# A new instruction order for the last three quarters of a fused attention and SwiGLU block

## The chip, the cores and the metric

The kernel runs on one core of a Trainium2 chip. The metric is the device time of one execution in microseconds (us). The kernel before was run three times: 239.23, 239.26 and 241.12 us, median 239.26.

A core has five engines that run their own instruction queues strictly in the order in which they were written and wait for each other through semaphores: TensorE (PE in the profile, with its weight loads as PEld), VectorE (DVE), ScalarE (ACT), GpSimd (POOL) and SyncE (SP), which here issues nearly all DMAs.

## The reference

2048 rows of 512 numbers pass an attention half and a feed-forward half, each with a layer norm that is scaled and shifted by a condition vector, and a gated residual:

```python
mod = (_silu(c) @ w_mod).reshape(c.shape[0], 6, 1, -1)
sa, ca, ga, sb, cb, gb = ...
h = _layernorm(x, axis=-1) * (1 + ca) + sa
x = x + ga * _A_ref(h, A_wqkv, A_wo)
h = _layernorm(x, axis=-1) * (1 + cb) + sb
x = x + gb * _B_ref(h, B_w1, B_w3, B_w2)
```

`_A_ref` is attention with 32 heads of 16, in which a row sees itself and seven earlier rows at a distance of 2, 4, ... 14. `_B_ref` is a SwiGLU: `(silu(h @ w1) * (h @ w3)) @ w2` with 1792 inner columns.

## The kernel before

The 2048 rows are 16 tiles of 128 (T = 0 to 15). The kernel is a list of 1118 operations, each with its engine, its instructions and what it reads and writes (`_build`, from line 273). Two lists at the end of the file say everything about their sequence. `ORDER` (line 980) has the operations' numbers in one global order; `Program.place` (line 143) deals them out to the five engines in that order, so it fixes each engine's queue. `SLOTS` (line 1027) has the buffer of each value that takes one from a pool: one of eight PSUM banks, or one of a few buffers for queries, normalized rows, shifted values, attention weights, FFN products and so on. From both, `Program.synchronize` (line 165) derives every semaphore wait: an operation waits for what it reads, and for the last users of the buffer that it takes over. A change of the two lists therefore moves operations within the queues and changes waits, and leaves each operation as it is.

The operations that the text names, by tile or row group:

- **lg T** (TensorE, line 752): 16 small matmuls that sum the products of query and shifted keys to logits, with the array split in four; VectorE makes the products before (**pq T**, line 742, 2.28 us).
- **at T** (TensorE, line 807): transposes of the softmaxed weights of tiles T and T+1; the softmax itself is some VectorE steps and an Exp on ScalarE.
- **value loads** (SP, line 124 in the profile, like every DMA): four DMAs of 256 KB for each tile bring the values, shifted by the eight distances, from a scratch in DRAM.
- **av T** (VectorE, line 827, 2.28 us): values times weights. **ac T** (TensorE, line 855): eight split matmuls that sum them; ScalarE copies the sum to SBUF (line 861), and a DMA, **ot T**, transposes it.
- **wo T** (TensorE, line 867): output projection, four matmuls; VectorE adds it to x (line 871).
- **second layer norm**: GpSimd and ScalarE (lines 586 to 601). For tiles 0 to 3 TensorE transposes the normalized rows (line 636). For the others a DMA transposes each tile (`sb_h<-sb_xn`) and four ScalarE instructions modulate a group (line 621).
- **F g.u** (TensorE, line 883): four matmuls with w1 (the gate) or with w3 (the other factor) for inner column block u (0 to 13) of row group g. Groups 0 and 1 are tiles 0-1 and 2-3, groups 2 and 3 tiles 4-7 and 8-11, groups 4 and 5 tiles 12-13 and 14-15; a matmul has 256 columns in groups 0, 1, 4, 5 and 512 in 2 and 3. ScalarE takes the SiLU (line 889), VectorE the product (line 892).
- **Z halves** (TensorE, line 921; line 909 for tiles 14 and 15): seven of the 14 matmuls with w2 of a tile; VectorE adds x (line 931) and SP stores the tile.

TensorE has enough independent work of the FFN to fill the time in which attention steps of other tiles wait for VectorE, ScalarE or a DMA. Which F or Z stands between which attention steps is written in `ORDER` and nowhere else.

Of the kernel before, what the change touches and what calls it, by code (L numbers as in the profile page):

```python
# [272 lines left out]
def _build(p, A_x, A_wqkv, A_wo, B_w1, B_w3, B_w2, c, w_mod, out):  # L273
# [720 lines left out]
    604, 311, 312, 269, 303, 317, 318, 386, 387, 309, 310, 388, 304, 401, 418, 605, 307, 308, 606, 389, 390, 607, 609, 608, 337,  # L994
    278, 315, 392, 313, 314, 322, 325, 445, 225, 338, 615, 610, 614, 616, 394, 611, 393, 613, 612, 305, 391, 328, 306, 329, 443,
    316, 444, 405, 406, 319, 617, 622, 626, 407, 446, 627, 395, 396, 397, 419, 420, 623, 477, 45, 634, 635, 447, 642, 618, 272, 320,
    46, 636, 637, 628, 629, 619, 620, 621, 52, 226, 326, 51, 630, 631, 408, 624, 625, 344, 638, 448, 421, 422, 50, 640, 639, 641,
    662, 670, 644, 643, 645, 449, 409, 646, 410, 450, 632, 647, 47, 633, 654, 398, 399, 451, 663, 666, 400, 671, 672, 452, 48, 343,
    650, 655, 668, 667, 669, 648, 649, 682, 683, 684, 453, 652, 651, 653, 435, 656, 657, 664, 433, 436, 685, 454, 665, 673, 658,
    678, 434, 437, 321, 426, 686, 687, 689, 695, 688, 694, 691, 660, 323, 659, 661, 423, 478, 475, 696, 424, 438, 425, 697, 690,  # L1000
    692, 674, 693, 742, 439, 730, 465, 731, 466, 468, 743, 427, 744, 745, 726, 706, 708, 707, 709, 476, 479, 467, 469, 428, 458,
    429, 710, 711, 456, 457, 712, 713, 722, 723, 724, 727, 728, 729, 455, 732, 733, 440, 725, 430, 746, 698, 699, 459, 53, 702, 703,
    480, 54, 470, 471, 472, 734, 735, 441, 442, 460, 461, 345, 346, 714, 431, 432, 738, 762, 462, 481, 497, 482, 473, 474, 483, 675,
    676, 747, 763, 463, 464, 704, 498, 484, 764, 765, 499, 715, 487, 716, 717, 700, 701, 718, 720, 509, 770, 771, 679, 705, 750,
    736, 737, 490, 748, 772, 485, 719, 500, 749, 488, 721, 739, 740, 752, 741, 507, 766, 767, 769, 489, 779, 768, 751, 754, 753,
    486, 501, 773, 774, 778, 775, 776, 780, 777, 781, 782, 491, 785, 758, 759, 760, 327, 783, 755, 529, 502, 510, 508, 492, 784,
    798, 818, 511, 512, 503, 531, 532, 680, 830, 493, 513, 330, 530, 831, 521, 539, 832, 514, 515, 820, 822, 814, 799, 815, 522,
    819, 504, 505, 516, 517, 541, 494, 324, 520, 495, 518, 506, 834, 806, 786, 807, 496, 761, 836, 794, 833, 823, 835, 677, 821,
    838, 858, 808, 859, 681, 533, 534, 559, 519, 523, 535, 809, 837, 540, 558, 542, 543, 524, 860, 525, 570, 790, 796, 795, 788,
    797, 545, 861, 791, 810, 787, 789, 802, 792, 793, 526, 544, 536, 547, 546, 549, 548, 862, 537, 569, 538, 550, 803, 527, 528,  # L1010
    839, 863, 864, 804, 805, 811, 551, 594, 812, 813, 866, 824, 825, 867, 800, 567, 593, 552, 553, 554, 874, 592, 868, 869, 826,
    557, 816, 560, 801, 840, 827, 870, 871, 555, 872, 568, 556, 817, 876, 841, 865, 854, 875, 561, 873, 846, 877, 828, 571, 842,
    595, 881, 562, 572, 829, 577, 563, 584, 855, 879, 578, 579, 564, 573, 850, 856, 580, 574, 878, 880, 906, 908, 581, 596, 565,
    566, 575, 576, 954, 857, 585, 907, 583, 909, 918, 919, 894, 582, 586, 843, 956, 955, 957, 886, 887, 958, 756, 898, 587, 588,
    895, 597, 890, 891, 589, 926, 847, 598, 599, 959, 960, 962, 899, 900, 901, 927, 961, 848, 590, 600, 591, 601, 1032, 910, 920,
    921, 963, 964, 965, 892, 893, 967, 966, 1034, 928, 1033, 1035, 1036, 1037, 851, 968, 852, 849, 972, 974, 976, 978, 973, 980,
    929, 911, 984, 986, 977, 979, 975, 844, 845, 985, 987, 853, 1039, 988, 990, 989, 1038, 930, 931, 932, 981, 982, 983, 933, 902,
    904, 991, 903, 905, 970, 934, 969, 1040, 896, 897, 971, 882, 1041, 888, 889, 884, 883, 922, 885, 923, 935, 936, 924, 946, 1043,
    1042, 942, 937, 938, 950, 1004, 1006, 1005, 1007, 1000, 1045, 1002, 1001, 925, 1008, 1012, 1009, 1013, 1016, 1017, 996, 998,
    997, 914, 999, 915, 1018, 992, 1003, 1044, 993, 994, 1014, 1015, 1019, 995, 916, 757, 912, 917, 1024, 913, 939, 1028, 940, 1070,  # L1020
    1090, 1071, 1086, 1072, 1073, 1091, 1010, 1087, 1074, 1011, 1082, 1075, 1088, 941, 1083, 1078, 1089, 1079, 1092, 1093, 1094,
    1084, 1096, 1095, 1097, 1080, 1081, 943, 951, 1085, 952, 944, 947, 948, 949, 1054, 1050, 1066, 1051, 1052, 1053, 953, 945, 1020,
    1062, 1064, 1076, 1077, 1063, 1046, 1067, 1068, 1069, 1047, 1055, 1056, 1057, 1021, 1022, 1023, 1058, 1060, 1059, 1061, 1029,
    1048, 1025, 1098, 1049, 1030, 1065, 1099, 1100, 1101, 1110, 1111, 1112, 1114, 1115, 1113, 1116, 1117, 1026, 1027, 1102, 1031,
    1103, 1104, 1105, 1106, 1107, 1108, 1109,
]
SLOTS = [
    7, 0, 1, 2, 3, 4, 5, 6, 0, 1, 2, 3, 4, 5, 6, 7, 0, 1, 2, 3, 4, 5, 6, 7, 0, 3, 4, 5, 6, 0, 1, 1, 0, 2, 3, 0, 4, 0, 7, 1, 0, 2, 1,
    2, 3, 6, 1, 5, 0, 7, 5, 7, 6, 2, 2, 1, 4, 0, 1, 3, 1, 2, 0, 4, 1, 4, 0, 7, 5, 1, 3, 6, 3, 0, 4, 2, 0, 1, 2, 1, 1, 0, 2, 4, 0, 1,
    2, 1, 4, 3, 6, 5, 1, 1, 0, 1, 3, 2, 3, 2, 4, 0, 0, 2, 3, 4, 1, 0, 3, 5, 6, 5, 1, 5, 3, 3, 2, 2, 0, 2, 6, 1, 2, 0, 3, 6, 7, 5, 3,  # L1030
    0, 1, 1, 0, 6, 0, 1, 1, 0, 0, 0, 0, 0, 1, 1, 5, 1, 6, 0, 1, 1, 1, 0, 5, 1, 0, 3, 1, 5, 0, 2, 3, 1, 4, 0, 2, 4, 2, 100, 5, 1, 2,
    5, 1, 1, 0, 1, 4, 0, 7, 1, 0, 4, 0, 1, 1, 1, 1, 5, 0, 7, 0, 0, 1, 1, 6, 0, 1, 1, 1, 0, 5, 1, 0, 0, 100, 7, 0, 2, 1, 1, 6, 0, 2,
    6, 2, 100, 5, 1, 1, 3, 1, 3, 0, 2, 5, 0, 4, 1, 0, 0, 1, 0, 1, 6, 0, 0, 6, 1, 0, 4, 1, 7, 0, 2, 6, 6, 1, 0, 0, 1, 1, 6, 100, 2,
    0, 0, 2, 1, 4, 7, 2, 1, 5, 103, 2, 102, 3, 101, 6, 103, 1, 100, 4, 101, 5, 104, 2, 106, 4, 102, 3, 100, 3, 105, 2, 104, 1, 102,
    4, 105, 1, 100, 3, 108, 5, 104, 2, 109, 4, 105, 7, 110, 5, 102, 7, 113, 5, 103, 6, 111, 2, 102, 6, 107, 6, 101, 1, 112, 0, 100,
    3, 102, 0, 3, 2, 0, 4, 4, 104, 0, 101, 1, 105, 1, 102, 1, 105, 7, 115, 1, 103, 4, 116, 7, 100, 2, 100, 5, 101, 7, 105, 7, 101,
    5, 119, 2, 102, 1, 117, 7, 100, 7, 118, 5, 103, 2, 103, 4, 100, 5, 106, 5, 104, 4, 114, 2, 102, 0, 104, 6, 104, 4, 107, 2, 101,
    0, 101, 2, 1, 4, 3, 1, 1, 105, 5, 113, 3, 100, 1, 100, 6, 101, 0, 112, 1, 103, 5, 115, 3, 101, 1, 101, 6, 100, 5, 110, 6, 100,
    7, 102, 0, 102, 1, 116, 4, 101, 5, 109, 3, 104, 6, 105, 3, 101, 5, 103, 0, 105, 7, 108, 4, 105, 0, 111, 7, 105, 7, 119, 1, 103,
    3, 100, 5, 102, 4, 103, 0, 1, 2, 4, 2, 3, 105, 5, 108, 6, 103, 7, 105, 6, 105, 4, 114, 4, 102, 1, 115, 7, 101, 4, 106, 7, 100,  # L1040
    4, 113, 7, 100, 0, 104, 7, 104, 1, 114, 1, 100, 4, 113, 7, 104, 0, 107, 6, 100, 1, 116, 0, 100, 3, 117, 0, 101, 3, 110, 2, 102,
    4, 109, 7, 100, 3, 102, 0, 101, 5, 103, 0, 3, 0, 6, 101, 0, 103, 2, 101, 0, 100, 4, 105, 5, 118, 2, 100, 1, 102, 3, 100, 7, 101,
    4, 105, 5, 112, 4, 103, 6, 108, 2, 100, 4, 119, 4, 103, 6, 104, 6, 101, 2, 111, 2, 105, 1, 100, 4, 102, 1, 105, 1, 101, 2, 106,
    3, 103, 0, 113, 2, 102, 6, 100, 1, 2, 1, 0, 102, 3, 116, 1, 103, 5, 118, 4, 104, 5, 110, 7, 100, 4, 114, 0, 101, 1, 117, 7, 105,
    7, 109, 4, 102, 4, 115, 7, 100, 5, 107, 7, 102, 1, 108, 4, 104, 7, 112, 7, 103, 1, 101, 1, 101, 4, 102, 1, 105, 4, 103, 5, 105,
    0, 100, 3, 101, 6, 103, 7, 101, 4, 103,
]


# [26 lines left out]
```

## Time and profile before

| | us |
|---|---|
| median of three runs | 239.26 |
| the profiled execution | 240.36 |
| its span | 238.6 |
| TensorE busy | 232.2 |
| VectorE busy | 179.4 |
| ScalarE busy | 138.3 |
| GpSimd busy | 28.8 |
| TensorE idle from 36 to 236 us | 2.05 |

The page divides the span into 40 slices of 6 us and gives the busy share of each in tenths. A timeline lists instructions of one engine in the order of time, like ones merged, with the engine's idle time before them in brackets and what ended it. Ends of matmuls are modelled, so a merged row's length runs a little past the start of the next one; distances are taken from start to start. For SP a row is the time of issuing; the landing comes later. Times in the text count from the start of the span.

### The profile page before, as it was taken

The numbers are of one execution on the slowest core, as the hardware profiler recorded it, in microseconds if no ns is written. First come the engines' busy times: TensorE is split into PE (matmuls) and PEld (weight loads), VectorE is DVE, ScalarE is ACT, GpSimd is POOL, SyncE is SP. The second block draws the span as 40 slices with busy tenths as digits, with TensorE's granted clock in tenths as the row PEclk, the third lists the DMA queues.
The fourth block names the chain that finished last, engine by engine and source line by source line (L and its number), as shares of the span: only waits on it lengthen the run. The fifth ranks groups of instructions, "written<-read, shape, count | busy, mean of one in ns | idle before, by whom it ended". The sixth has DMA issues, their size and how long they took to land.

```text
span 238.6 us, 4560 instructions
## 1 busy us (share of the span) xinstructions
PE 232.2 (97%) x1806; PEld 136.7 (57%) x1806; DVE 179.4 (75%) x279; ACT 138.3 (58%) x267; POOL 28.8 (12%) x66
## 2 busy tenths in 40 slices
PE   7999999999999998999999999999899999999995
PEld 4776554545688683664444444444375457485874
DVE  5699999999999999899999999690653403434433
ACT  2289587899978737776765594747553406040300
POOL 4434000013002000240003420020010000000000
PEclk9999999999999999999999999999999999999999
DMA  6999999999999996876972783634303000000202
GB/s 216 372 330 309 157 242 301 217 288 315 302 293 254 247 203 178 240 180 193 229 220 62 192 209 76 166 113 46 67 5 104 3 0 0 3 22 0 69 1 88
DMA packets 46317, 38.85 MB, mean 163 GB/s; under 512 B 21704, under 2 KB 37080, under 8 KB 46296
## 3 DMA queue, kind: packets, MB, share of 16 engines
q1 hardware_dynamic: 46288, 38.56, 65.1%
q8 instruction: 14, 0.23, 0.4%
q14 instruction: 7, 0.06, 0.1%
q10 hardware_dynamic: 8, 0.00, 0.0%
HBM read 29.62 MB, written 4.21 MB: 142 GB/s over the span
## 4 chain that ended last, share of the span: by engine, by line
PE 83%; DMA 8%; DVE 3%; SPq 3%; ACT 1%; issue 0%
PE pall L883 40%; PE pall L921 17%; PE pall L691 7%; PE pall L867 5%; DMA sb_x<-in_A_x_dram 5%; PE pall L711 4%; DMA sb_ot<-sb_ac 3%; PE pall L752 3%; SPq L124 3%; PE pall L855 3%; PE pall L909 3%; DVE sb_pq L742 2%; DVE sb_st L555 1%; PE pall L807 1%; DVE sb_xn L576 1%; ACT sb_ac L861 0%
## 5 line engine op out<-in xcount | busy, mean ns | idle before, releaser
L883 PE MATMUL pall<-sb_h,sb_w 128*128 128x256 bf16 (+1 forms) x672 | 102.6, 308 | 0.0
L883 PEld LDWEIGHTS pall<-sb_h,sb_w 128*128 128x128 bf16 x672 | 65.0, 98 | 35.7 <-issue 2.5
L889 ACT ACTIVATE sb_sg<-pall 128x256 bf16<-128x256 f32 (+1 forms) x84 | 35.6, 454 | 54.5 <-PE pall L883 53.4
L892 DVE TENSOR_TENSOR sb_hh<-sb_sg,pall 128x256 bf16<-128x256 bf16 (+1 forms) x84 | 40.0, 505 | 36.1 <-PE pall L883 34.0
L921 PE MATMUL pall<-sb_w,sb_hh 128*128 128x512 bf16 x196 | 44.9, 379 | 0.0
L742 DVE TENSOR_TENSOR sb_pq<-sb_q,sb_kT 128x4096 bf16<-128x4096 bf16 x16 | 36.3, 2282 | 0.0
L921 PEld LDWEIGHTS pall<-sb_w,sb_hh 128*128 128x128 bf16 x196 | 19.0, 98 | 21.6 <-DVE sb_hh L892 0.4
L691 PE MATMUL pall<-sb_h,sb_wqkv 128*128 128x512 bf16 (+1 forms) x160 | 31.0, 336 | 0.0
L827 DVE TENSOR_TENSOR sb_vsh<-sb_vsh,sb_al 128x4096 bf16<-128x4096 bf16 x12 | 27.2, 2284 | 0.5 <-DMA sb_vsh<-v_scratch_dram 0.5
L621 ACT ACTIVATE sb_h<-sb_h,sb_modc 128x512 bf16<-128x512 bf16 (+1 forms) x24 | 16.5, 743 | 9.1 <-DMA sb_h<-sb_xn 9.1
L691 PEld LDWEIGHTS pall<-sb_h,sb_wqkv 128*128 128x128 bf16 x160 | 14.7, 98 | 11.7 <-ACT sb_ac L861 0.4
L931 DVE TENSOR_TENSOR sb_o<-pall,sb_x 128x512 bf16<-128x512 f32 (+1 forms) x18 | 11.1, 628 | 10.9 <-PE pall L921 7.1
L867 PE MATMUL pall<-sb_wo,sb_ot 128*128 128x512 bf16 x64 | 16.0, 379 | 1.9 <-DMA sb_ot<-sb_ac 1.9
L711 PE MATMUL pall<-sb_wqkv,sb_h 128*128 128x512 bf16 x64 | 16.0, 379 | 0.0
L644 ACT ACTIVATE sb_h<-pall,sb_modc 128x256 bf16<-128x256 bf16 (+1 forms) x18 | 9.9, 611 | 7.9 <-DVE sb_modc L509 6.9
L586 POOL TENSOR_SCALAR sb_nm<-sb_sx 128x2 f32<-128x2 f32 x8 | 1.7, 218 | 105.3 <-DVE sb_x L871 105.3
L861 ACT ACTIVATE sb_ac<-pall 128x512 bf16<-128x512 f32 x16 | 9.5, 595 | 7.1 <-PE pall L855 6.9
L601 ACT ACTIVATE sb_xn<-sb_x,sb_nb,sb_rs 128x512 bf16<-128x512 bf16 x16 | 12.4, 807 | 0.7 <-POOL sb_nb L599 0.6
L871 DVE SCALAR_TENSOR_TENSOR sb_x<-pall,sb_x 128x512 bf16<-128x512 f32 x16 | 10.8, 686 | 2.2 <-PE pall L867 2.1
L590 ACT ACTIVATE sb_xn<-sb_x,sb_nm 128x512 bf16<-128x512 bf16 x16 | 11.4, 714 | 1.8 <-POOL sb_nm L586 1.8
L721 ACT ACTIVATE sb_v<-pall 128x512 bf16<-128x512 f32 x16 | 9.6, 605 | 2.8 <-PE pall L711 2.8
L555 DVE BATCH_NORM_STATS2 sb_st<-sb_x 128x6 f32<-128x512 bf16 x16 | 10.5, 679 | 0.7 <-DMA sb_x<-in_A_x_dram 0.6
(87 smaller groups left out, 209.5 us busy)
## 6 DMA issues: line engine op xcount, KB each, us to landing
sb_vsh<-v_scratch_dram SPq DMA_DIRECT2D x48, 256.0 KB, 5.2
sb_vshx<-v_scratch_dram SPq DMA_DIRECT2D x16, 256.0 KB, 4.4
sb_w<-in_B_w_dram SPq DMA_DIRECT2D x6, 512.0 KB, 7.6
sb_w<-in_B_w_dram SPq DMA_DIRECT2D x6, 384.0 KB, 4.2
v_scratch_dram<-sb_v SPq DMA_DIRECT2D x16, 128.0 KB, 6.1
out_dram<-sb_o SPq DMA_DIRECT2D x14, 128.0 KB, 1.8
sb_wqkv<-in_A_wqkv_dram SPq DMA_DIRECT2D x6, 256.0 KB, 6.3
sb_x<-in_A_x_dram SPq DMA_DIRECT2D x4, 256.0 KB, 6.5
```

The lines of the kernel that those rows point to most:

```text
L555: o = p.op("dve", lambda e, T=T: e.bn_stats(st[:, T, :], x_sb[:, T, :]), 595, ("st", T), r=[vx[T]], w=[vs])
L601: p.op("act", lambda e, vn=vn, T=T: e.activation(vn.at[:], x_sb[:, T, :], ACT.Identity, bias=nb[:, T, :], scale=rs[:, NT + T, :]), c_act(5 ...
L621: return e.activation(vh.at[:, ft, 0:n * P], vh.at[:, ft, 0:n * P], ACT.Identity, bias=modc[:, 8 * which + ft:8 * which + ft + 1], scale=m ...
L691: ins = e.matmul(bank(vp)[:, j * n:(j + 1) * n], wqkv[:, t, col:col + P], vh.at[:, t, 0:n], start=(t == ORDER[0] and j == 0), stop=(t == O ...
L711: ins = e.matmul(bank(vp), vh.at[:, t, tt * P:(tt + 1) * P], wqkv[:, t, 2 * D:3 * D], start=(t == ORDER[0]), stop=(t == ORDER[-1]))
L742: return e.tensor_tensor(vp.at[:], in0, in1, ALU.mult)
L827: return e.tensor_tensor(v_w, v_w, a_w, ALU.mult)
L867: ins = e.matmul(bank(vy), vt.at[:, ft, :], wo[:, ft, :], start=(ft == 0), stop=(ft == KT - 1))
L883: ins = e.matmul(bank(vp)[:, 0:n], wt[:, t, fi * P:(fi + 1) * P], vh.at[:, t, 0:n], start=(t == 0), stop=(t == KT - 1))
L889: p.op("act", lambda e: e.activation(vt.at[:, 0:n], bank(vgp)[:, 0:n], ACT.Silu), c_act(n), k, r=[vgp], w=[vt], table="silu")
L892: p.op("dve", lambda e: e.tensor_tensor(vh_.at[:, 0:n], vt.at[:, 0:n], bank(vup)[:, 0:n], ALU.mult), c_dve(n), k, r=[vt, vup], w=[vh_])
L921: ins = e.matmul(bank(vz), vhh[fi].at[:, tt * P:(tt + 1) * P], w2[:, fi, :], start=(fi == 0), stop=(fi == NF - 1))
```

## The change

441 of the 1118 places of `ORDER` stay as they are; the remaining 677 hold the same numbers in another sequence. In the engines' queues the first difference comes at place 145 of 384 on TensorE (67.1 us of the profile), 103 of 263 on VectorE, 91 of 241 on ScalarE, 68 of 168 on SP and 40 of 62 on GpSimd. `SLOTS` differs in 400 of 655 places. No operation is added, removed or altered.

```diff
@@ -994,56 +994,56 @@
     316, 444, 405, 406, 319, 617, 622, 626, 407, 446, 627, 395, 396, 397, 419, 420, 623, 477, 45, 634, 635, 447, 642, 618, 272, 320,
-    46, 636, 637, 628, 629, 619, 620, 621, 52, 226, 326, 51, 630, 631, 408, 624, 625, 344, 638, 448, 421, 422, 50, 640, 639, 641,
...
+    46, 636, 637, 628, 629, 619, 620, 621, 52, 226, 326, 51, 630, 631, 408, 662, 663, 638, 639, 666, 643, 632, 646, 640, 647, 648,
...
 SLOTS = [
...
-    2, 3, 6, 1, 5, 0, 7, 5, 7, 6, 2, 2, 1, 4, 0, 1, 3, 1, 2, 0, 4, 1, 4, 0, 7, 5, 1, 3, 6, 3, 0, 4, 2, 0, 1, 2, 1, 1, 0, 2, 4, 0, 1,
...
+    2, 3, 6, 1, 5, 0, 7, 5, 7, 6, 2, 2, 1, 4, 0, 1, 3, 1, 2, 0, 4, 1, 4, 0, 7, 0, 1, 3, 6, 3, 0, 4, 2, 5, 1, 2, 1, 1, 0, 2, 4, 0, 1,
...
```

Read as operations, these are the passages of the queues that the text speaks of (`x2` is both halves in a row; `Z 0b` is the second half of tile 0):

```
TensorE, from the first difference
before  F0.1 F0.5 at4 F0.5 F0.11 F0.13 F0.6 wo3 F0.7 F0.3 F0.9 wo2 F0.12 F0.13 F0.8 F0.12 F0.7 at6 ...
after   F0.11 F0.5 F0.12 F0.3 F0.7 F0.5 F0.7 F0.6 F0.1 wo2 wo3 F0.10 F0.12 F0.11 F0.8x2 F0.9 at4 F0.13 at6 ...

TensorE, tiles 4 to 7
before  ac7 F1.9 wo5 ac6 F1.4 wo4 F1.10 wo7 Z0b wo6
after   ac7 F1.12 F1.1 F1.9 F1.1 F1.0 wo5 ac6 F1.12 F1.10 wo4 F1.4x2 F1.0 wo7 Z0b wo6

TensorE, to the first F of group 2
before  wo6 F1.1 F1.4 F1.0 F1.5x2 Z1b F1.13 F1.9 F1.12 at8 F1.10 F1.13 Z2a Z3a Z3b Z2b ac9 lg11 lg10 ac8 F2.3
after   wo6 F1.5x2 at8 F1.9 Z1b F1.13x2 F1.10 Z2a Z3a Z3b Z2b ac8 lg10 ac9 lg11 F2.13

TensorE, tiles 10 and 11
before  ac11 lg12 lg13 ac10 F2.1 F2.2
after   lg13 lg12 ac10 ac11 F2.11 F2.8 F2.5

TensorE, tiles 12 and 13
before  ac12 ac13 Z7b Z6a at14 F3.6x2 wo12 wo13
after   ac13 ac12 at14 Z4b Z5b wo13 F3.4 wo12

TensorE, tiles 14 and 15
before  ac14 ac15 F3.2 F3.11 Z5b F3.4 wo14 wo15
after   ac15 ac14 F3.8 F3.4 F3.5x2 F3.0 F4.5x2 F4.1 F4.0x2 F3.0 F3.3 wo15 wo14

ScalarE, second layer norm of tiles 4 to 7 (sq: squares, nm: normalizing, mod: modulation; SiLUs left out)
before  sq4 sq5 sq6 sq7 nm5 nm4 nm6 nm7 mod x4
after   sq4 sq5 nm4 nm5 sq6 sq7 nm6 nm7 mod x4

SP (w1, w3: weight loads of 384 KB; v: value loads, one quarter each; hT: transposes of normalized rows)
before  ot3 w3 w1 ot2 w3 v5x4 ...       after  ot3 ot2 w3 w1 w3 v5x4 ...
before  ot7 ot6 v9x3 v8x2 v9 v8x2 hTx4
after   ot7 v9 ot6 v8 v9x2 (store of tile 15's values) v9 v8x2 hT v8 hTx3
```

## The prediction

> **What bounds the kernel now.** I read the page first (busy shares, slices), then stretches of the span, then the waits of TensorE, its timeline at each wait, the chain of waits, and the queues that feed those places. The page, busy time and slices:
>
> ```profile
> PE 232.2 (97%) x1806; PEld 136.7 (57%) x1806; DVE 179.4 (75%) x279; ACT 138.3 (58%) x267; POOL 28.8 (12%) x66
> ...
> PE   7999999999999998999999999999899999999995
> ...
> DVE  5699999999999999899999999690653403434433
> ...
> PEclk9999999999999999999999999999999999999999
> ```
>
> TensorE is busy nearly all the time at full clock. VectorE is nearly as full until slice 27 (160 us) and has room afterwards. Stretches of the span behind the point where the order starts to differ (columns: busy us and instructions of PE, PEld, DVE, ACT, POOL; clock; DMA share; GB/s):
>
> ```profile
> 67.00:110.00 43.00, 41.77 (x351) 27.90 (x349) 41.11 (x62) 29.79 (x62) 5.25 (x12) 1.00 0.93 219
> 110.00:160.00 50.00, 50.00 (x358) 23.21 (x356) 47.36 (x56) 32.54 (x55) 6.97 (x10) 1.00 0.64 169
> 160.00:236.00 76.00, 75.19 (x497) 47.01 (x495) 29.13 (x59) 25.93 (x58) 2.88 (x7) 1.00 0.13 31
> ```
>
> So TensorE stands still for 43.00 - 41.77 = 1.23 us, 0 and 0.81 us: 2.04 us in 169. The timeline of TensorE has them (last column: idle before it, and what ended it):
>
> ```profile
> 92.04 0.61 PE L855 MATMUL pall<-sb_vsh,sb_ind 128*32 128x512 bf16 x8 [0.19 <-DVE sb_vsh L827]
> ...
> 95.54 1.02 PE L867 MATMUL pall<-sb_wo,sb_ot 128*128 128x512 bf16 x4 [1.04 <-DMA sb_ot<-sb_ac]
> ```
>
> ```profile
> 168.35 1.04 PE L867 MATMUL pall<-sb_wo,sb_ot 128*128 128x512 bf16 x4 [0.81 <-DMA sb_ot<-sb_ac]
> ```
>
> The chain of waits (start, us, what) shows what the two long ones hang on:
>
> ```profile
> 89.89 0.57 PE pall L855 x8
> 90.49 0.60 ACT sb_ac L861
> 91.12 4.29 DMA sb_ot<-sb_ac
> ...
> 164.07 0.49 ACT sb_ac L861
> 164.59 3.71 DMA sb_ot<-sb_ac
> ```
>
> A tile's summed values (ac) are copied by ScalarE and transposed by a DMA before its output projection (wo). What sits between ac and wo on TensorE hides this chain, or doesn't.
>
> **What the order can win.** The set of instructions, their shapes and the first 67 us are unchanged, so the matmul time is fixed. From rows: an F (four matmuls) takes 0.437 us from start to start with 256 columns and 0.863 with 512, a Z half 1.51, wo 0.863, ac and lg 0.44, at 0.22.
>
> *Tiles 6 and 7.* From the start of ac7 (89.82) to wo7 (95.54) the chain takes 5.7 us. The new order has ten F, wo5, ac6 and wo4 between them: 0.55 + 10 x 0.437 + 2 x 0.863 + 0.55 = 7.2 us. The 1.04 us goes. ac6, which waited 0.19 us for VectorE's av6, now stands 3.6 us behind ac7's start (0.55 + 5 F + wo5) instead of 2.2, and VectorE's work ahead of av6 is the same by its rows: that goes too.
>
> *Tiles 14 and 15.* From ac15 (161.86) to wo15 (168.35) it took 6.5 us, because ScalarE's copy came only at 164.07. The new order puts ac14, seven F of group 3 and five of group 4 there: 0.44 + 0.55 + 7 x 0.863 + 5 x 0.437 = 9.2 us. The 0.81 us goes.
>
> *Changes between the four-fold tiled matmuls (lg, ac) and full ones.* Each costs 0.1 us (F to lg 0.53 from start to start against 0.437; ac to F 0.54 against 0.44). There are 18 of them in the old order behind 67 us and 16 in the new one: -0.2 us.
>
> Together -2.24 us, and that is about all there is: a start, a tail and a matmul total that this change doesn't touch.
>
> **What the new order exposes.** I went through the new queues with the same rows, asking at each step that waits for another engine whether the work put ahead of it is as long as the chain it waits for. "Due" below is where a step stands when the rows ahead of it in its own queue are added up from 67.1 us without waits.
>
> *The first F of group 2.* It needs tiles 4 to 7 normalized again: residual, statistics, four transposes on the DMA queue, four modulations on ScalarE. The rows of before, from the queue's and ScalarE's timelines:
>
> ```profile
> 102.79 5.23 SPq L124 DMA_TRANSPOSE sb_h<-sb_xn  x4
> ```
>
> ```profile
> 109.16 2.93 ACT L621 ACTIVATE sb_h<-sb_h,sb_modc 128x512 bf16<-128x512 bf16 x4 [2.95 <-DMA sb_h<-sb_xn]
> ```
>
> wo6 ended at 98.94 and the modulations at 112.09: 13.1 us. TensorE had 10 F, at8, five Z halves, two ac and two lg in between (4.37 + 0.22 + 7.56 + 1.9 = 14.0 us), enough. The new order leaves six F: 12.3 us, 0.8 short. At the same place a quarter of tile 8's value load has been put behind the first of those four transposes on SP's queue. The transpose can't issue before its row is normalized, about 101 us by ScalarE's new sequence; so that quarter issues at 102.2 and lands 5.0 later (these loads: median 4.4 to 5.2) at 107.2, where av8 is due at 105.7. av8 then ends at 109.5, its pq11 behind it at 111.7, and lg11, due at 111.2, waits 0.5. lg11 and the first F stand next to each other, so most of it is the same wait: I take 1.1 us for both, 0 if ScalarE's new sequence ends the chain sooner, 1.8 if both add up.
>
> *Tile 13.* The chain ac to landed transpose took 148.68 to 153.20 = 4.5 us for tile 12, the nearest case. The new order has only ac12, at14 and two Z halves between ac13 and wo13: 0.44 + 0.54 + 0.22 + 3.02 = 4.2 us (before: 6.4, with two Z halves, at14, two F and wo12). 0.3 us; 0 to 2.3, by tile 15's 6.5.
>
> *ac10, ac11.* Their banks are needed by the second and third F behind them, while ScalarE has a SiLU and a normalization queued before those copies: 0.3 us; 0 to 0.9 (0.6 is one 512-column copy more).
>
> *Weight loads behind ot2.* SP's queue of before:
>
> ```profile
> 62.36 1.23 SPq L124 DMA_TRANSPOSE sb_ot<-sb_ac  x1
> 63.64 1.12 SPq L124 DMA_DIRECT2D sb_w<-in_B_w_dram  x2
> 64.81 1.20 SPq L124 DMA_TRANSPOSE sb_ot<-sb_ac  x1
> ```
>
> The two loads of 384 KB in the middle now come after ot2, which can't start before 64.7, and issue at 66.0 and 66.6 instead of 63.64 and 64.27. They took 4.2 and 4.7 us to land; the new order asks for the second at 72.7 (F0.10: 67.1 + 9 F + wo2 + wo3). 66.6 + 4.7 = 71.3: nothing, since 1.4 us of F cover it. Without that cover, at the 7.1 us of the load behind them, 1.0 us. ot2 itself loses two loads ahead of it and stays in time for 71.0.
>
> *All other steps* keep at least 0.3 us by these sums: 0.2 us for those that don't; 0 to 0.5.
>
> Behind 172 us all is F and Z with VectorE and ScalarE mostly idle, in both orders; the nearest row is the third stretch above, where 0.81 us in 76 was idle, all of it at wo15. The last piece of TensorE is a half of tile 14 in both, with one addition and one store after it: 0.
>
> Sum: -2.24 + 1.1 + 0.3 + 0.3 + 0 + 0.2 = -0.34 us. The profiled execution took 240.36 us around its span of 238.6; it would take 240.0, with a span of 238.3. The runs have a median of 239.26, 1.1 below the profiled one; the same difference gives **238.9 us**.
>
> **Rivals.**
>
> *All holes close and none opens:* -2.24, 237.0 us. For it: each of the new waits is below 1.2 us and rests on a chain that ScalarE's or VectorE's order may shorten. Against: four F fewer ahead of group 2 are counted, not guessed.
>
> *The old waits are this execution's own:* the runs lie between 239.23 and 241.12, and the profiled one 1.1 above the median, so the median run may stand still for only half of the 2.04 us. Then -1.1 - 0.2 + 1.9 = +0.6: 239.9 us. For it: both long waits are for a DMA, whose landing varies (these transposes 2.4 to 6.6 us). Against: the distances before wo7 and wo15 are short by rows of ScalarE too.
>
> *Slower: tile 8's values come late.* One quarter of a load sits behind a transpose that waits for ScalarE. Landing of these loads goes up to 11.3 us in the trace. At 8.5 us it would land at 110.7; av8 would end at 112.9, ac8, due at 109.8, would wait 3.1 us, lg11 0.8 more, and with the 0.8 of the other places the net is -2.24 + 4.7 = +2.5: 241.7 us. It decides from a landing of about 8.4 us on. For it: VectorE has no idle time to make up with (41.11 of 43 us busy). Against: tile 8's other quarters in that stretch landed in 4.6 to 5.7 us.
>
> TensorE's idle stretches here are at most 1.04 us and the granted clock stays 1.00. The Trainium skill, "TensorE: Matmul & The Clock Gate" (section on the HAM clock gate), says that an idle window of some 3.4 us halves the clock for about as long; no run here shows it behind 67 us. By it, the last rival would be dearer from a landing of 8.8 us on, by an estimated 1.7 us (3.4 us at half clock), and the forecast would be the same.
>
> **Numbers.** About 1% (2.4 us) is what a measurement of this kernel can tell from no change. Forecast 238.9: chance 0.41. 237.0: 0.25. 239.9: 0.16. 241.7 or more: 0.17. Faster than 236.87 would need more than every idle TensorE microsecond: 0.01. The first three lie within 1%: 0.82 the same, 0.17 slower. The range goes from 237.0 to 241.5: the first three cases with the upper bounds of the priced waits (1.8 + 0.9 + 1.0 + 0.5, and 0.3 for tile 13, whose 2.3 was tile 15's late copy: 4.5 - 2.24 = +2.3, 241.5).
>
> **What will show it.** The waits of TensorE should have no L867 wait at wo7 and wo15; a wait of some 1 us before lg11 or the first 512-column F near 111 us; 0.3 us at wo13. VectorE should stand idle before av8. If TensorE's idle sum behind 67 us is above 4 us, the pairwise sums have missed a chain that feeds itself; if it is below 0.5, ScalarE's new sequence has shortened the chain to group 2.

## The result, and the profile after

| | before | after |
|---|---|---|
| median, us | 239.25 (238.44 to 241.12, 6 runs) | 242.24 (241.45 to 242.91, 6 runs) |
| the profiled execution, its span | 240.36, 238.6 | 242.32, 240.6 |

The new order is slower: the ratio is 1.0114, with a 95% interval of 1.0073 to 1.0155. Run again beside other runs of before it was 242.63 us and 1.009 (1.0057 to 1.0122). So it costs 2 to 3 us; the forecast was 238.9, in a range up to 241.5. Medians here and below are over all executions of a kernel, ratios over those that did not run some per cent longer at a lower mean clock.

The page of after, busy time and slices:

```profile
PE 229.7 (95%) x1780; PEld 135.9 (56%) x1806; DVE 178.6 (74%) x279; ACT 139.7 (58%) x267; POOL 30.8 (13%) x66
...
PE   7899999999999999978999999998899999999995
...
DVE  5689999999999999969999999554535431225522
```

TensorE has new dents at slices 18 and 19 (102 to 114 us) and at 28 (from 162 us); slice 29 read 8 before too, for wo15's wait. VectorE has a new one at slice 18. GpSimd's busy time rose from 28.8 to 30.8 us with the same 66 instructions: its steps took longer, and there are no more of them. That is the first hint of the cause. The clock stayed full (1.00 in every stretch below). The stretches (busy us and instructions of PE, PEld, DVE, ACT, POOL; clock; DMA share; GB/s):

```profile
67.00:110.00 43.00, 40.70 (x344) 27.74 (x348) 40.02 (x62) 29.66 (x60) 6.62 (x12) 1.00 0.88 224
110.00:160.00 50.00, 49.37 (x351) 23.09 (x356) 44.32 (x54) 31.72 (x51) 5.08 (x8) 1.00 0.64 156
160.00:238.00 78.00, 75.80 (x494) 47.15 (x499) 32.89 (x63) 28.22 (x63) 5.46 (x8) 1.00 0.13 38
```

What is left of each stretch is 2.30, 0.63 and 2.20 us here, 1.23, 0 and 0.81 before. Part of the new figures is no idleness: 26 matmul records are missing in this trace. The view of TensorE's waits from 67 us on is cleaner (what is waited for; us in total, times, longest):

```profile
PE pall L921 <- DVE sb_hh L892: 2.1, 1, 2.1
PE pall L883 <- ACT sb_h L621: 1.0, 1, 1.0
PE pall L855 <- ACT sb_sg L889: 0.6, 1, 0.6
```

No line 867 is left: the waits of wo7 and wo15 are gone. In their place a Z half (Z3b, 108.92 us) waits 2.1 us for an FFN product, ac15 (167.67) 0.6 us for ScalarE to read a bank, and the first F of group 4 (174.25) 1.0 us for modulated rows: 3.7 us. The chain of waits says what the long ones hang on:

```profile
101.24 1.42 ACT sb_xn L590 x4
103.79 2.25 POOL sb_nb L599
106.06 1.52 ACT sb_xn L601 x2
108.92 2.97 PE pall L921 x13
...
160.60 1.53 ACT sb_xn L590 x4
163.20 2.83 POOL sb_rs L597
167.14 1.46 ACT sb_sg L889 x3
169.32 2.29 DMA sb_h<-sb_xn
174.25 2.36 PE pall L883 x20
```

Both holes begin at a GpSimd step on two numbers per row (lines 597 and 599), the statistics of the second layer norm, and it takes over 2 us. GpSimd's timeline around the first of them:

```profile
102.73 0.19 POOL L596 TENSOR_SCALAR sb_rs<-sb_var 128x2 f32<-128x2 f32 x1 [2.16 <-ACT sb_xn L590]
103.01 0.70 POOL L597 TENSOR_TENSOR sb_rs<-sb_rs,sb_cst 128x2 f32<-128x2 f32 x1
103.79 2.24 POOL L599 TENSOR_TENSOR sb_nb<-sb_nm,sb_rs 128x2 f32<-128x2 f32 x1
```

VectorE's timeline over the same time:

```profile
103.69 2.29 DVE L827 TENSOR_TENSOR sb_vshx<-sb_vshx,sb_al 128x4096 bf16<-128x4096 bf16 x1
107.88 0.75 DVE L892 TENSOR_TENSOR sb_hh<-sb_sg,pall 128x256 bf16<-128x256 bf16 x2 [1.91 <-ACT sb_sg L889]
108.55 2.28 DVE L827 TENSOR_TENSOR sb_vsh<-sb_vsh,sb_al 128x4096 bf16<-128x4096 bf16 x1
```

And ScalarE's:

```profile
106.06 1.52 ACT L601 ACTIVATE sb_xn<-sb_x,sb_nb,sb_rs 128x512 bf16<-128x512 bf16 x2 [2.39 <-POOL sb_nb L599]
107.48 0.36 ACT L889 ACTIVATE sb_sg<-pall 128x256 bf16<-128x256 f32 x1
```

Read together: VectorE begins av9 at 103.69. GpSimd's last step, 0.20 us when undisturbed, begins 0.10 us later and ends at 106.03, just behind av9 (105.98). ScalarE stands 2.39 us before the normalization of tiles 6 and 7 (nm6, nm7), and the new order has put that ahead of the SiLU of F1.13. So that SiLU ends at 107.84, VectorE stands 1.91 us before F1.13's product with F1.10's queued behind it, and Z3b, which needs both, starts 2.1 us late. The same chain of tiles 6 and 7 before, in GpSimd's timeline (the step of line 597 between the two took its usual 0.69 us):

```profile
101.62 1.58 POOL L596 TENSOR_SCALAR sb_rs<-sb_var 128x2 f32<-128x2 f32 x1 [0.70 <-ACT sb_xn L590]
...
104.05 0.20 POOL L599 TENSOR_TENSOR sb_nb<-sb_nm,sb_rs 128x2 f32<-128x2 f32 x1
```

There the first step is the long one (1.58 us), and the SiLU of F1.13 stood ahead of the normalization in ScalarE's queue.

The second hole, in GpSimd's timeline:

```profile
162.20 0.91 POOL L596 TENSOR_SCALAR sb_rs<-sb_var 128x2 f32<-128x2 f32 x1 [1.64 <-ACT sb_xn L590]
163.20 2.82 POOL L597 TENSOR_TENSOR sb_rs<-sb_rs,sb_cst 128x2 f32<-128x2 f32 x1
```

Here av14 ran on VectorE from 163.16 to 165.45. ScalarE's timeline:

```profile
166.32 0.81 ACT L601 ACTIVATE sb_xn<-sb_x,sb_nb,sb_rs 128x512 bf16<-128x512 bf16 x1 [3.58 <-POOL sb_nb L599]
```

ScalarE stood 3.58 us before the normalization of tile 13, with three SiLUs of group 3 behind it in its queue; one of them had to empty ac15's bank, and the transposes of tiles 12 and 13 left late.

ScalarE's row of the normalization in the table of groups (last: idle before it, and what ended it), before:

```profile
L601 ACT ACTIVATE sb_xn<-sb_x,sb_nb,sb_rs 128x512 bf16<-128x512 bf16 x16 | 12.4, 807 | 0.7 <-POOL sb_nb L599 0.6
```

and after:

```profile
L601 ACT ACTIVATE sb_xn<-sb_x,sb_nb,sb_rs 128x512 bf16<-128x512 bf16 x16 | 12.3, 806 | 7.6 <-POOL sb_nb L599 7.5
```

The work is the same, 16 instructions in 12.3 us. What is new is 7 us of standing still for GpSimd, and an order behind it in which that matters.

### The profile page after: what moved, and what is told of

Its sections match the earlier page's. It is cut to its first block, busy times and chain, and to the rows that moved or that the text cites. A ratio compares the mean times of both kernels' runs of the same rounds, so it can differ in the third digit from the quotient of the medians.

```text
span 240.6 us, 4530 instructions
## 1 busy us (share of the span) xinstructions
PE 229.7 (95%) x1780; PEld 135.9 (56%) x1806; DVE 178.6 (74%) x279; ACT 139.7 (58%) x267; POOL 30.8 (13%) x66
## 4 chain that ended last, share of the span: by engine, by line
PE 80%; ACT 7%; POOL 4%; DMA 3%; DVE 2%; issue 2%; SPq 0%
PE pall L883 35%; PE pall L921 15%; PE pall L691 9%; PE pall L711 5%; PE pall L867 5%; PE pall L752 3%; PE pall L855 3%; PE pall L909 3%; DMA sb_wm_s<-in_w_mod_dram 3%; ACT sb_xn L601 2%; ACT sb_xn L590 2%; POOL sb_nb L599 2%; POOL sb_rs L597 2%; ACT sb_sg L889 1%; DMA sb_h<-sb_xn 1%
## 5 line engine op out<-in xcount | busy, mean ns | idle before, releaser
L889 ACT ACTIVATE sb_sg<-pall 128x256 bf16<-128x256 f32 (+1 forms) x84 | 36.7, 452 | 48.6 <-PE pall L883 44.4
L921 PE MATMUL pall<-sb_w,sb_hh 128*128 128x512 bf16 x188 | 43.7, 379 | 2.5 <-DVE sb_hh L892 2.1
L691 PE MATMUL pall<-sb_h,sb_wqkv 128*128 128x512 bf16 (+1 forms) x154 | 30.2, 335 | 0.8 <-DVE sb_st L555 0.4
L827 DVE TENSOR_TENSOR sb_vsh<-sb_vsh,sb_al 128x4096 bf16<-128x4096 bf16 x11 | 25.0, 2284 | 0.1
L586 POOL TENSOR_SCALAR sb_nm<-sb_sx 128x2 f32<-128x2 f32 x8 | 2.4, 299 | 116.0 <-DVE sb_x L871 116.0
L601 ACT ACTIVATE sb_xn<-sb_x,sb_nb,sb_rs 128x512 bf16<-128x512 bf16 x16 | 12.3, 806 | 7.6 <-POOL sb_nb L599 7.5
L711 PE MATMUL pall<-sb_wqkv,sb_h 128*128 128x512 bf16 x62 | 15.5, 379 | 0.2
L867 PE MATMUL pall<-sb_wo,sb_ot 128*128 128x512 bf16 x61 | 15.0, 379 | 0.1
L827 DVE TENSOR_TENSOR sb_vshx<-sb_vshx,sb_al 128x4096 bf16<-128x4096 bf16 x5 | 11.4, 2286 | 0.1
```

Of the source, the lines that this page charges most:

```text
L601: p.op("act", lambda e, vn=vn, T=T: e.activation(vn.at[:], x_sb[:, T, :], ACT.Identity, bias=nb[:, T, :], scale=rs[:, NT + T, :]), c_act(5 ...
L691: ins = e.matmul(bank(vp)[:, j * n:(j + 1) * n], wqkv[:, t, col:col + P], vh.at[:, t, 0:n], start=(t == ORDER[0] and j == 0), stop=(t == O ...
L711: ins = e.matmul(bank(vp), vh.at[:, t, tt * P:(tt + 1) * P], wqkv[:, t, 2 * D:3 * D], start=(t == ORDER[0]), stop=(t == ORDER[-1]))
L827: return e.tensor_tensor(v_w, v_w, a_w, ALU.mult)
L867: ins = e.matmul(bank(vy), vt.at[:, ft, :], wo[:, ft, :], start=(ft == 0), stop=(ft == KT - 1))
L889: p.op("act", lambda e: e.activation(vt.at[:, 0:n], bank(vgp)[:, 0:n], ACT.Silu), c_act(n), k, r=[vgp], w=[vt], table="silu")
```

## The experiments

Theory A: a GpSimd step that begins while a 2.28 us VectorE product of two SBUF operands runs is held to the product's end; two such holds, and a SiLU placed behind the held step on ScalarE, are the whole loss. Against it stand the rivals that the expectations state where they use them, above all that the places which the prediction had priced (value load, wo13, the banks of ac10 and ac11, weight loads) are the loss, and that the waits for GpSimd only cover them.

The instructions of the first 67 us are the same in all kernels, yet they took 66.8 to 70.6 us in the profiled executions, with late first loads or a lower clock before 20 us. Beside the ratio I therefore give the *rest*: from TensorE's first differing place to the end of the span. It was 171.58 us in the profile of before and 173.31 in that of after.

### The new order once more

> The changed kernel once more, beside the others. If its three new TensorE waits belong to the order (Z3b at 108.8 us for a VectorE product 2.1 us, ac15 0.6, the first F of group 4 1.0), they stand at the same places within 0.3 us each and the time is 242.2 us. If they are accidents of one execution (rival), they stand elsewhere or sum to less than 2 us.

The ratio was 1.009 (1.0057 to 1.0122), the rest 173.06 us, with the same three waits: 2.1, 0.5 and 1.1 us. The step of line 599 took 2.24 us again, that of line 597 2.73. It is no accident of one execution.

### The old order once more

> The kernel before once more, for a second profile. If its waits at wo7 and wo15 belong to the order, they stand there again with 0.7 to 1.3 us each and the time from the first differing piece to the end is 171.6 us within 0.3. If they were accidents, they are gone or elsewhere, and it is near 170 us.

238.5 us, rest 169.99. TensorE's waits from 67 us on:

```profile
PE pall L867 <- DMA sb_ot<-sb_ac: 0.3, 1, 0.3
PE pall L855 <- DVE sb_vsh L827: 0.3, 1, 0.3
```

wo7 didn't wait at all, wo15 0.3 us. Of the 2.04 us that the new order was to win, 1.4 belonged to the one execution that I had read.

### The SiLU ahead of the normalization

```diff
 ScalarE
-nm6 nm7  SiLU F1.13
+SiLU F1.13  nm6 nm7
```

> In the changed order, ScalarE's SiLU of F1.13 moves ahead of the two normalizations of tiles 6 and 7. Theory A (the SiLU stood in ScalarE's queue behind normalizations that wait for GpSimd, and held VectorE's queue and so Z3b): the Z3b wait of 2.1 us is gone, but the chain to the first F of group 2 is as long as before and now shows there (modulations end near 113.1 us, the first F is due at 111.7), so only 0.5 to 0.9 us is won: 241.5 us. Rival B (VectorE is simply behind with its work, by the late value load of tile 8): Z3b still waits, 242.2 us.

This missed. The ratio was 1.0121 (1.0065 to 1.0176), the median 245.17 us, the rest 175.42. Z3b's wait was gone, but the first F of group 2 waited 4.0 us for its modulated rows.

> The SiLU of F1.13 alone, once more, since most executions of its first run had a late start at a lower clock. Theory A: Z3b does not wait, the first F of group 2 waits 1 to 2 us for the modulations, and the time from the first differing piece to the end is 172.3 to 172.9 us (173.2 without the edit). If the 3.7 us wait at group 2 of its first profile belongs to the edit (rival: the transposes are slower when ac8 releases the loads behind them sooner), it stands there again and the time is 175 us.

The ratio was 1.02 (1.0133 to 1.0268), the rest 176.13 us. TensorE's timeline:

```profile
110.77 0.61 PE L752 MATMUL pall<-sb_pq,sb_E 128*32 128x256 bf16 x16
115.05 9.20 PE L883 MATMUL pall<-sb_h,sb_w 128*128 128x512 bf16 x34 [3.67 <-ACT sb_h L621]
```

The hold on GpSimd remained (2.24 us in both), so nm6 still started at 105.70. Moving the SiLU out from behind it saved Z3b's wait and left the group 2 chain as late as before. On top of that the fourth transpose of that chain took 4.3 us from issue to landing in both profiles, against 2.4 in both profiles of the new order, and in this profile the clock fell behind the wait (both in the last section). So of the two outcomes named, the rival's came: the wait stands there again. Theory A's rest of 172.3 to 172.9 was missed by 3.5 us, of which the transpose is 1.9 and the clock 1.7. The SiLU's place is what makes Z3b wait, as theory A has it, but moving it alone doesn't close the hole.

### The SiLU and the hold

```diff
 ScalarE
-nm6 nm7  SiLU F1.13
+SiLU F1.13  nm6 nm7
 VectorE
-av9  product F1.13  product F1.10
+product F1.13  product F1.10  av9
```

> As the run before, and VectorE's products of F1.13 and F1.10 move ahead of av9, so that GpSimd's last step for tiles 6 and 7 no longer starts under a 2.28 us VectorE product. Theory A with GpSimd held by that product: the step takes 0.2 us instead of 2.24, the normalizations start near 104.1 instead of 106.1, neither Z3b nor the first F of group 2 waits, 2.1 us is won: 240.1 us. If GpSimd's step is long for another reason (rival): it stays near 2.2 us wherever it starts, and the time is that of the run before, 241.5 us.

241.01 us, 1.004 (1.0004 to 1.0076), rest 171.43. GpSimd's timeline now:

```profile
102.96 0.70 POOL L597 TENSOR_TENSOR sb_rs<-sb_rs,sb_cst 128x2 f32<-128x2 f32 x1
103.74 0.20 POOL L599 TENSOR_TENSOR sb_nb<-sb_nm,sb_rs 128x2 f32<-128x2 f32 x1
```

With av9 moved behind the two products the step takes 0.20 us, and Z3b doesn't wait. What the prediction had put there came out from under it. VectorE's timeline and TensorE's:

```profile
107.30 2.29 DVE L827 TENSOR_TENSOR sb_vsh<-sb_vsh,sb_al 128x4096 bf16<-128x4096 bf16 x1 [0.41 <-DMA sb_vsh<-v_scratch_dram]
```

```profile
111.85 0.62 PE L752 MATMUL pall<-sb_pq,sb_E 128*32 128x256 bf16 x16 [0.63 <-DVE sb_pq L742]
112.78 4.48 PE L883 MATMUL pall<-sb_h,sb_w 128*128 128x512 bf16 x20 [0.32 <-ACT sb_h L621]
```

av8 waits for the quarter behind the transpose, lg11 0.63 and the first F 0.32 us. So the rival is right for about 1 us, which in the changed kernel is covered by Z3b's 2.1.

### The hold without the SiLU

```diff
 VectorE
-av9  product F1.13  product F1.10
+product F1.13  product F1.10  av9
```

> The changed order with one edit on VectorE alone: av9 behind the products of F1.13 and F1.10; ScalarE's queue is left as it is. GpSimd's last step for tiles 6 and 7 then starts with no 2.28 us product running. If that product is what held it, the step takes 0.2 us instead of 2.24, the normalizations start near 104 instead of 106, and Z3b hardly waits, although the SiLU still stands behind them. av9 and av8 then end 2 us later by VectorE's own rows, so ac8 waits about 1.3 and lg11 0.7 us instead, and the time to the end stays near 173 us. If the step is long for another reason, it stays near 2.2 us and Z3b waits as before.

241.85 us in a single execution, rest 173.08: no gain, as theory A had it. The step took 0.20 us and Z3b didn't wait, but VectorE now stood 2.06 us before F1.13's product, whose SiLU still came behind nm6 and nm7, with av9 and av8 queued behind:

```profile
105.44 0.75 DVE L892 TENSOR_TENSOR sb_hh<-sb_sg,pall 128x256 bf16<-128x256 bf16 x2 [2.06 <-ACT sb_sg L889]
```

TensorE's three longest waits:

```profile
PE pall L855 <- DVE sb_vsh L827: 1.2, 1, 1.2
PE pall L883 <- ACT sb_h L621: 1.0, 1, 1.0
PE pall L752 <- DVE sb_pq L742: 0.7, 1, 0.7
```

The 2.1 us moved to ac8 and lg11 (the F that waits 1.0 us is still that of group 4, behind the second hold). Both edits are needed, each on its own gains nothing.

### The second hold

```diff
 TensorE
-gate of F3.4  wo12  second half of F3.4
+wo12  gate and second half of F3.4
 ScalarE
-SiLU F3.4  squares of tiles 12, 13
+squares of tiles 12, 13  SiLU F3.4
```

> In the changed order, wo12 goes ahead of the gate half of F3.4 on TensorE, and F3.4's SiLU behind the squares of tiles 12 and 13 on ScalarE. Theory A at the second place (GpSimd's power step for tiles 12 and 13 started just as av14 began and was held by it for 2.8 us, and ScalarE's SiLUs and the transposes behind it): the chain starts 0.5 to 0.9 us sooner, the step falls ahead of av14 and takes 0.7 us, the waits of ac15 (0.6) and of the first F of group 4 (1.0) are gone: 240.6 us. Rival (the waits come from the transposes or from av14's late values): both waits stay, 242.2 us.

240.82 us, 1.0036 (0.9998 to 1.0073), rest 171.23. GpSimd's two steps now end before av14 begins:

```profile
165.48 0.70 POOL L597 TENSOR_TENSOR sb_rs<-sb_rs,sb_cst 128x2 f32<-128x2 f32 x1
166.26 0.19 POOL L599 TENSOR_TENSOR sb_nb<-sb_nm,sb_rs 128x2 f32<-128x2 f32 x1
```

VectorE's timeline shows what keeps av14 back:

```profile
166.65 2.29 DVE L827 TENSOR_TENSOR sb_vshx<-sb_vshx,sb_al 128x4096 bf16<-128x4096 bf16 x1 [1.30 <-DMA sb_vshx<-v_scratch_dram]
```

Counted from the first differing piece the whole chain, av15 too, comes 1.0 us earlier than in the new order, but av14 waits 1.30 us for its values. Had they been there, av14 would, by an estimate from these rows and the chain's usual pace, have begun about 0.2 us ahead of line 597's step, and held it. So this edit passes the hold only because a load is late. It also brings two things at once: an earlier start (1.0 us) and no hold (2.1 us). No run parts them; the 1.6 us of the two waits is more than the start alone.

The waits of ac15 and of the first F of group 4 are gone, Z3b's 2.1 us stays. Against the two profiles of the new order the rest is 1.8 to 2.1 us shorter; the two waits were 1.6.

### Both holds

> The edits of the two runs before it together (SiLU of F1.13 and its product ahead, wo12 ahead of F3.4) on the changed order. Each of them alone shortened the time from the first differing TensorE piece to the end from 173.2 us to 171.3. If the two losses stand apart (theory A), the gains add: about 169.5 us from there to the end, some 3.5 us less than the changed kernel and 1.5 to 2 less than the kernel before. If both edits merely cured one and the same lateness of VectorE (rival), the second adds nothing: 171.3.

The edits of the last experiment and of the one with SiLU and av9 together: 239.39 us, 0.998 (0.9954 to 1.0006), rest 171.13. All three waits of the changed kernel are gone, and with them the loss: this order can't be told from the old one. The rest missed the expected 169.5 by 1.6 us: lg11 waits 0.6, and there is a wait for which the prediction had only a bound (1.0 us), in TensorE's timeline:

```profile
76.02 1.05 PE L883 MATMUL pall<-sb_h,sb_w 128*128 128x256 bf16 x8 [0.82 <-DMA sb_w<-in_B_w_dram]
```

That is F0.8's second half, for the third weight load, which the two loads put behind ot2 push back. It landed at 75.97; in the profiles of the unmended new order it landed at 74.5 to 74.8, in time.

```diff
 SP
-ot3 ot2 w3 w1 w3
+ot3 w3 w1 ot2 w3
```

> As e4_both, and on SP's queue the two 384 KB weight loads go back ahead of ot2, as in the kernel before. In e4_both's profile the second half of F0.8 waited 1.0 us for the load behind them. If moving them behind ot2 costs that (the bound the prediction gave it, 1.0 us), the wait is gone and the time from the first differing TensorE piece to the end is 170.0 us, 0.997 of the kernel before or less. If that wait is only one execution's late DMA (rival), nothing changes: 0.998, and profiles of either order may show it.

With the two loads ahead of ot2 again the last one landed at 73.02, and F0.8 didn't wait: 239.95 us, 0.9982 (0.9944 to 1.0019), rest 170.24. Mended in three places the new order is as fast as the old one, not faster.

### Is there anything to win?

The old order, with wo7 moved behind Z0b and wo15 behind two more halves of F, and the product of Z0b ahead of wo7's residual on VectorE:

```diff
 TensorE
-wo7 Z0b wo6 ... wo14 wo15 F x4
+Z0b wo7 wo6 ... wo14 F x2 wo15 F x2
```

> The kernel before, with wo7 behind the second half of Z0 and wo15 behind two more F of group 3, so that the two DMA chains it waited for are covered; nothing else of the new order. If those waits belong to the old order in most executions, 0.7 us is won at wo7 (Z0's second half itself is ready only 0.5 us after its turn) and 0.8 to 1.0 at wo15: 170.0 us from the first moved piece to the end instead of 171.6, 1.5 us less than before. If they were accidents of the one profiled execution (the third case of the prediction), the gain is under 0.5 us.

239.88 us, 1.0003 (0.9969 to 1.0037), rest 170.21: no gain. The rest alone would look like the 170.0 of the first case, but the second profile of the unchanged old order has 169.99. The two waits went, and Z0b, now earlier, met another one, in TensorE's timeline:

```profile
94.85 1.69 PE L921 MATMUL pall<-sb_w,sb_hh 128*128 128x512 bf16 x7 [0.40 <-DVE sb_w L952]
```

It needs w2, which VectorE scales at that time (line 952).

### The SiLU's place in the old order

```diff
 ScalarE, order before
-SiLU F1.13  Exp products of at8  nm6 nm7
+Exp products of at8  nm6 nm7  SiLU F1.13
```

> The kernel before with the SiLU of F1.13 put behind the two normalizations, as the new order has it; nothing else. In the old order VectorE comes to that product only after pq10, near 106 to 107 us, and GpSimd's steps take their 0.2 to 1.6 us, so the SiLU is done by then: VectorE waits 0 to 0.3 us and no Z waits, 170.0 to 171.6 us from the first differing piece to the end. If a SiLU behind normalizations is costly in itself (rival), a Z half of tile 3 waits 1 us or more.

238.24 us in a single execution, rest 169.72: harmless. There a GpSimd step is held too (line 596, 1.49 us), but VectorE comes to F1.13's product only at 105.72, with the SiLU done. What hurts in the new order is the pair: a held step, and a SiLU that is wanted at once behind it.

The rests side by side, with TensorE's waits behind 67 us that can be named:

| | rest, us | waits, us |
|---|---|---|
| before, two profiles | 171.58, 169.99 | wo7 1.0, ac6 0.2, wo15 0.8; ac6 0.3, wo15 0.3 |
| after, two profiles | 173.31, 173.06 | Z3b 2.1, ac15 0.6, F of group 4 1.0; 2.1, 0.5, 1.1 |
| SiLU and av9 moved | 171.43 | lg11 0.6, F of group 2 0.3, F of group 4 1.1 |
| second hold mended | 171.23 | Z3b 2.1 |
| both | 171.13 | F0.8 0.8, lg11 0.6 |
| both, loads ahead | 170.24 | lg11 0.3, F of groups 2 and 4 0.5 |

A is confirmed for the first chain, where each edit was also made without the other: mending both chains takes away the three waits and the whole difference. For the second chain the earlier start isn't parted from the hold. The priced places are worth 1 us at lg11 and 0.8 at the weight load, and neither shows in the changed kernel.

## Why the prediction was wrong, by its steps

**The step that failed** is "All other steps keep at least 0.3 us by these sums: 0.2 us for those that don't; 0 to 0.5". All three waits of the changed kernel are among those other steps, and they measured 3.7 us. The sums took each step's duration from the old order as if it stayed the same beside other neighbours. They gave GpSimd's steps no price of their own: the chain of 13.1 us to group 2 is the old one whole, with its step of 1.58 us in it. And they followed the normalization of tiles 6 and 7 only to the transposes and modulations, never the SiLU behind it into VectorE's queue and on to Z3b. The row that should have stopped me stands in the table of groups of before, below the rows that its page prints:

```profile
L599 POOL TENSOR_TENSOR sb_nb<-sb_nm,sb_rs 128x2 f32<-128x2 f32 x8 | 4.9, 618 | 0.6
```

An undisturbed one takes 0.20 us, not the mean of 618 ns. Four of the eight second-norm chains of before have a held step in their trace, the longest 2.10 us; I didn't ask what the holds depend on.

**The gain was over-sized.** The waits at wo7, ac6 and wo15 did go, as predicted. But together they were 2.04 us in the one profile and 0.6 in the second: most of the 2.04 belonged to the one execution, and that this was the one profiled is luck. The rival "the old waits are this execution's own" was right in this: it reckoned with half of the 2.04 us, and 0.6 us was left.

**The priced waits were right in mechanism and in size where they could be seen.** lg11 and the first F of group 2 had 1.1 us; they measured 0.63 + 0.32 once Z3b no longer covered them. The quarter of tile 8's values was to land at 107.2, and av8 waited for it until 107.30 in the kernel with SiLU and av9 moved. The rival with late values named this place, but needed a load of 8.5 us, which none of these profiles shows there. The weight loads, taken at 0 with a bound of 1.0, cost 0 in the changed kernel and 0.8 in one of its variants. wo13 and the banks of ac10 and ac11 had 0.6 us together and cost nothing.

**The account.** New waits 3.7, old ones not paid 0.6, two fewer mode switches 0.2 (by the prediction's estimate; no run parts them): 3.7 - 0.6 - 0.2 = +2.9 us; the medians differ by 2.99 and, in the second comparison, 2.73. With the old waits of the first profile it would be +1.5, and the rests of the two first profiles do differ by only 1.73. The forecast of -0.34 missed by 1.4 on the gain (2.04 against 0.6) and by 1.8 on the new waits (1.9 against 3.7).

**The signs it named.** The waits of wo7 and wo15 are gone, as it said. A wait at lg11 or the first F of group 2, 0.3 us at wo13 and an idle VectorE before av8 were not to be seen in the changed kernel. Idle time above 4 us was to mean that "the pairwise sums have missed a chain that feeds itself". The stretches leave 5.1 us, but missing records are in that; the named waits are 3.7, and each of the three gaps of 0.2 us that the profile names "issue" stands before a group of F with one matmul record missing. So the threshold isn't clearly passed, though such a chain is what had been missed.

## What to carry to other kernels

When an order is re-planned, check for each small GpSimd step which long VectorE product with two SBUF operands may run beside it, and price the step by its worst row in the trace, not by its usual one. In a queue that runs in order, follow a delay through everything queued behind the delayed instruction, on into the next engine's queue; don't stop at the consumer you had in mind. Before pricing a gain at the waits of one profile, read a second one: here 1.4 of 2.04 us weren't there.

## What the runs showed of the hardware

**A GpSimd step is held by a VectorE product.** In all 13 profiles the steps of lines 596, 597 and 599 took 0.19, 0.70 and 0.20 us when no product of line 742 or 827 was running as they began. Begun during one, they ended 0.05 to 0.6 us behind its end and took, for instance, 0.91, 1.58, 2.10, 2.24 and 2.82 us; the nine that began within 0.1 us of its end took their usual time. Line 586's step is held too, 0.86 us instead of 0.22 in the new order, under VectorE's step of line 952 (0.95 us, two operands in SBUF). Who begins first decides, to 0.1 us: line 599 began 0.10 us behind av9 and took 2.24; in the kernel with both holds mended it began 0.09 us ahead of av14 and took 0.20. The Trainium skill, "SBUF — State Buffer" (sections "Who interferes with whom" and "Summary: rules for kernel authors"), says that a VectorE instruction with two SBUF inputs contends with a GpSimd instruction that reads SBUF, and that the later of the two waits until the first has finished. All these rows agree.

**The clock fell behind an idle stretch, not always.** The stretches around the 3.67 us wait (columns as above):

```profile
110.00:114.00 4.00, 1.38 (x44) 0.77 (x35) 3.96 (x6) 1.94 (x3) 0.00 (x0) 1.00 0.70 210
114.00:118.00 4.00, 2.95 (x8) 1.04 (x9) 3.72 (x3) 3.95 (x7) 0.00 (x0) 0.64 0.61 153
118.00:122.00 4.00, 4.00 (x19) 1.83 (x18) 2.41 (x4) 1.75 (x2) 0.00 (x0) 0.93 0.58 146
```

At 0.64 and 0.93 of full clock, 0.36 x 4 + 0.07 x 4 = 1.72 us of clock are missing, which is 3.4 us at half speed: the trace's clock record has 0.5 from 115.12 us for 3.41 us. The F behind the wait were 1.69 us later than in after, counted from the first of them. In the other profile of the same kernel a wait of 3.98 us left the clock at 1.00. The Trainium skill, "TensorE: Matmul & The Clock Gate" (section on the HAM clock gate), speaks of an idle window of some 3.4 us in a free-running count. The size of the loss agrees, and that about the same idle time cost it once and once not fits a window whose phase isn't fixed. With the clock the wait of 3.67 us cost 5.4.

**A transpose landed late beside an instruction fetch.** In the kernel with only the SiLU moved the fourth transpose of normalized rows took 4.3 us to land in both profiles, in the new order 2.4. In the second of these profiles its last data packet ended at 109.66, 2.4 us ahead of its landing. Of the 32 packets of 4 bytes that follow the data, 30 began within 0.2 us. The last two began at 110.77 and 110.78, as a 16 KB instruction fetch, on the DMA engines since 109.54, ended (110.79). The first profile has the same: the fetch from 113.81 to 114.87, the last two packets at 114.86 and 114.87, the landing at 116.11. In both profiles of the new order no fetch falls there, all 32 packets begin within 0.2 us, and the landing follows 0.3 us behind the last. So the fetch stands ahead of the last packets in both late cases. That it holds them wasn't tested, and why the landing came another 1.3 us behind them stays open.
